# Loading by partition halves on two DMA queues: K, V and weight loads of a decode layer

## The chip, the core and the metric

The kernel runs on one core of one Trainium2 chip. The metric is the device time in microseconds (us) of one execution, the median over several executions. A profile is one further execution taken by the hardware profiler; its span runs from the first to the last instruction on the core, and the execution's own device time is a little longer than its span.

Five engines run beside each other: TensorE (PE, with its weight loads listed as PEld), VectorE (DVE), ScalarE (ACT), GpSimd (POOL) and SyncE (SP). SP and ACT each issue DMAs to a queue of their own; both queues are served by the core's 16 DMA engines.

## What is computed

One decode step of a transformer layer for 4 sequences, one token each, in bfloat16: LayerNorm, attention over the last 2048 positions of a cache with 32 query heads and 4 key/value heads of size 128, then LayerNorm and a gated feed-forward block.

```python
W = min(4096, max(256, Sk // 4))            # 2048
q = (layernorm(x) @ wq).reshape(B, 1, 32, 128)
k = repeat(k_cache[:, :, Sk - W:, :], 8)    # B, 4 -> 32 heads
v = repeat(v_cache[:, :, Sk - W:, :], 8)
p = softmax(q @ k.T * 128 ** -0.5)
h = x + (p @ v).reshape(B, 1, 4096) @ wo
hn = layernorm(h)
out = h + (silu(hn @ w1) * (hn @ w3)) @ w2
```

Shapes: x is 4 x 1024, wq 1024 x 4096, wo 4096 x 1024, w1 and w3 1024 x 3584, w2 3584 x 1024, and each cache gives 4 sequences x 4 heads x 2048 x 128. Every byte of these is read from HBM once, 55.6 MB in all.

## The kernel before

**Where data stands.** One tile, `ring`, takes 160 KiB of each of the 128 partitions. The list `plan` (L128 to L146) says in which order loads are issued and at which place of the ring each lands, in units of `KIB` = 512 elements, which is 1 KiB per partition. `load_next` (L150) issues the next entries of the plan. All of these are issued on SP's queue: wq in two parts, then K of batches 0 to 3, V of batches 0 to 3, wo, w1, w3 in two parts, and w2 in four parts of 17, 7, 3 and 1 rows. A batch of K or V is 2 MB; wo is 8 MB, w1 and w3 7 MB each, w2 7 MB. A load that lands on a place used before waits until the matmuls that read the old data are done, so the calls of `load_next` stand behind those matmuls: `load_next(8)` at the start (L159) covers the plan to the first V entry, one call stands in the wq loop (L267), one in the K loop at its eighth step (L327), two in the PV loop after batches 1 and 3 (L386), one after row 12 of wo (L413), one after wo (L414), and three loads at once in the w1 loop (L463). In SP's own instruction stream they simply follow each other, each with its waits; SP does nothing else. The framework also gives its DMAs eight completion semaphores in turn, so a DMA waits until the eighth one before it has landed.

A DMA of 128 partitions has one contiguous row per partition: 16 KB for a batch of K or V, 64 KB for wo, 56 KB for w1, 28 KB for each half of w3.

**The moved columns.** `CE` = 512 (L111): the last CE columns of the last of a partition's eight wq rows are left out of the tail load (`load_tail`, L122) and come by three small loads (`load_side`, L114) as tiles of 20, 12 and 12 partitions. The projection then adds eight small matmuls for them (L268 to L275). The number of bytes is the same either way; what changes is which DMA engine brings them.

**The order of the work.** Projection q (L251), then 16 steps of the K loop (L309): in each, 16 transposes of K on PE, one copy of half of the result from PSUM by DVE (L319) and one by ACT (L321), and four score matmuls of the step before (L300). Softmax follows (L331 to L357), the PV product over 4 batches x 64 blocks (L376), wo (L403), LayerNorm (L417 to L445), w1 (`gate_up("w1")`, L465), the gate's exponential and reciprocal on ACT and DVE, w3 (`gate_up("w3")`, L472), the product and its transpose on DVE (L474, L477), w2 (L483) and the output.

Of the kernel before, what the change touches and what calls it, by code (L numbers as in the profile page):

```python
# [10 lines left out]
P = 128  # L11
# [8 lines left out]
def kernel(  # L20
# [13 lines left out]
    nc = tc.nc  # L34

    B, _, D = A_x.shape
    Hkv, Sk, Dh = A_k_cache.shape[1], A_k_cache.shape[2], A_k_cache.shape[3]
    Hq = A_wq.shape[1] // Dh
    REP = Hq // Hkv
    W = min(4096, max(256, Sk // 4))  # L40
    F = B_w1.shape[1]
    KC = D // P
    NSB = W // 512
# [30 lines left out]
    PK = P // Hkv  # L74
    JK = W // PK
# [3 lines left out]

    RING = 5 * 16384  # L80
    RQ = 4
    BS = 2
    wq_v = A_wq.rearrange("(p i) n -> p (i n)", i=KC)
    wo_v = A_wo.rearrange("(p i) n -> p (i n)", i=IO)
    w1_v = B_w1.rearrange("(p i) n -> p (i n)", i=KC)
    w3_v = B_w3.rearrange("(p i) n -> p (i n)", i=KC)
    w2_v = B_w2.rearrange("(p i) n -> p (i n)", i=IF)
    ring = stream.tile([P, RING], BF16)
# [4 lines left out]
        nc.sync.dma_start(out=t, in_=src[:, r0 * n : (r0 + m) * n])  # L93
        return [t[:, k * n : (k + 1) * n] for k in range(m)]

    def load_kv(at, src, b):

        out = []
        for k in range(BS):
            v = ring[:, at + k * JK * Dh : at + (k + 1) * JK * Dh]  # L100
            nc.sync.dma_start(
                out=v,
                in_=src[b + k, :, Sk - W : Sk, :].rearrange("g (pp j) d -> pp g (j d)", pp=PK),
            )
            out.append(v.rearrange("p (j d) -> p j d", d=Dh))
        return out

    N_Q, N_F = Hq * Dh, F


    CE = 512  # L111
    SETS = [(0, 5, 4), (80, 3, 2), (104, 3, 2)]

    def load_side(r0, ne, ns):  # L114

        t = ktpool.tile([P, JG * QD * 16], BF16, tag="kT")
        rows = A_wq[r0 * KC : (r0 + ne * 4 * ns) * KC, N_Q - CE : N_Q]
        rows = rows.rearrange("(t i k) n -> k i t n", i=ne, k=KC)[KC - 1]
        nc.sync.dma_start(out=t[: ne * 4, : ns * CE], in_=rows)  # L119
        return [t[: ne * 4, k * CE : (k + 1) * CE] for k in range(ns)]  # L120

    def load_tail(at, src, n, r0, m):  # L122

        t = ring[:, at : at + m * n]
        nc.sync.dma_start(out=t[:, : m * n - CE], in_=src[:, r0 * n : (r0 + m) * n - CE])
        return [t[:, k * n : (k + 1) * n] for k in range(m)]
    KIB = 512
    plan = [  # L128
        ("wq", load_rows, (0, wq_v, N_Q, 0, 4)),
        ("side", load_side, SETS[0]),  # L130
        ("side", load_side, SETS[1]),
        ("side", load_side, SETS[2]),
        ("wq", load_tail, (32 * KIB, wq_v, N_Q, 4, 4)),
        ("k", load_kv, (64 * KIB, A_k_cache, 0)),
        ("k", load_kv, (96 * KIB, A_k_cache, 2)),
        ("v", load_kv, (128 * KIB, A_v_cache, 0)),
        ("v", load_kv, (0, A_v_cache, 2)),
        ("wo", load_rows, (32 * KIB, wo_v, D, 0, 32)),
        ("w1", load_rows, (96 * KIB, w1_v, N_F, 0, 8)),
        ("w3", load_rows, (0, w3_v, N_F, 0, 4)),  # L140
        ("w3", load_rows, (28 * KIB, w3_v, N_F, 4, 4)),
        ("w2", load_rows, (56 * KIB, w2_v, D, 0, 17)),
        ("w2", load_rows, (90 * KIB, w2_v, D, 17, 7)),
        ("w2", load_rows, (104 * KIB, w2_v, D, 24, 3)),
# [5 lines left out]
    def load_next(n=1):  # L150
        for _ in range(n):
            if cursor[0] < len(plan):
                kind, f, args = plan[cursor[0]]
                loaded.setdefault(kind, []).extend(f(*args))
                cursor[0] += 1

    x_sb = act.tile([B, D], BF16)
    nc.scalar.dma_start(out=x_sb[:], in_=x_flat)
    load_next(8)  # L159

    ident = const.tile([P, P], BF16)
    make_identity(nc, ident[:])
# [12 lines left out]
    for c in range(2):  # L175
# [8 lines left out]
        out=xn[:], in0=x_sb[:], scalar1=mv[:, 0:1], scalar2=rstd[:, 0:1],  # L184
# [14 lines left out]
    for r0, ne, ns in SETS:  # L199
        v = xn[:, r0 * KC : (r0 + ne * 4 * ns) * KC]  # L200
        v = v.rearrange("b (s l i k) -> b k l i s", s=4, l=ns, i=ne)
        nc.vector.tensor_copy(
            out=xs[:, len(sl) : len(sl) + ns, : ne * 4].rearrange("b l (i s) -> b l i s", s=4),
            in_=v[:, KC - 1, :, :, :],
        )
        for l in range(ns):
            nc.tensor.transpose(
                out=ts_ps[: ne * 4, len(sl), :], in_=xs[:, len(sl), : ne * 4], identity=ident[:B, :B]
# [4 lines left out]
    for _, ne, ns in SETS:  # L213
# [14 lines left out]
        out=perm[:].rearrange("p (h dq) -> p h dq", dq=JG),  # L228
        in_=ident[:].rearrange("p (dq h) -> p h dq", dq=JG),
# [12 lines left out]
    for j in range(2, JG):  # L242
        nc.vector.tensor_tensor(
            out=same[:, 0, :], in0=same[:, 0, :], in1=ident[:, j * QD : (j + 1) * QD], op=ALU.add
# [6 lines left out]
    for kc in range(KC):  # L251
        wq_t = loaded["wq"][kc]
        for hf in range(CQ // 512):
            for g in range(JG):
                c0 = g * CQ + hf * 512
                n = min(512, N_Q - CE - c0) if kc == KC - 1 else 512
                if n <= 0:
                    continue
                nc.tensor.matmul(  # L259
                    q_ps[QD * g : QD * g + B, hf * 512 : hf * 512 + n],  # L260
                    lhsT=xnT[:, kc, :],
                    rhs=wq_t[:, c0 : c0 + n],
                    start=(kc == 0),
                    stop=(kc == KC - 1 or (kc == KC - 2 and c0 + 512 == N_Q)),
                )
        if kc == RQ - 1:
            load_next()  # L267
            for k, np_ in enumerate(sl):  # L268
                nc.tensor.matmul(
                    q_ps[QD * (JG - 1) : QD * (JG - 1) + B, CQ - CE : CQ],  # L270
                    lhsT=xsT[:np_, k, :],
                    rhs=loaded["side"][k],
                    start=False,
                    stop=False,
                )  # L275
    q_sb = act.tile([P, CQ], BF16)
    nc.vector.tensor_single_scalar(out=q_sb[:, :512], in_=q_ps[:, :512], scalar=qscale, op=ALU.mult)  # L277
# [2 lines left out]
    for r in range(REP):  # L280
        nc.tensor.transpose(out=qt_ps[:, r, :], in_=q_sb[:, r * Dh : (r + 1) * Dh], identity=ident[:])
    nc.vector.tensor_copy(
        out=qz[:, :, : Hkv * QD].rearrange("p b (g z) -> p b g z", g=Hkv)[:, :, :, :REP],
        in_=qt_ps[:].rearrange("p r (g x) -> p x g r", g=Hkv)[:, :B, :, :],
# [10 lines left out]
    def emit_scores(u):  # L295
        b, n = units[u]
        kT_v = kT_tiles[u][:].rearrange("d j (pp g) -> d g j pp", g=Hkv)
        for g in range(Hkv):
            z0 = (b * Hkv + g) * QD
            nc.tensor.matmul(  # L300
                scores_ps[QD * g : QD * (g + 1), n * 512 : (n + 1) * 512],
                lhsT=qz_v[:, z0 : z0 + QD],
                rhs=kT_v[:, g, :, :],
                start=(b == 0),
                stop=(b == B - 1),
            )

    nt = 0
    for u, (b, n) in enumerate(units):  # L309
        k_v = loaded["k"][b]  # L310
        kT = ktpool.tile([P, NJ, P], BF16, tag="kT")
        for t in range(NJ // TB):
            kt_ps = psA.tile([P, TB, P], BF16, tag=f"kt{nt % 4}")
            for jj in range(TB):
                nc.tensor.transpose(  # L315
                    out=kt_ps[:, jj, :], in_=k_v[:, n * NJ + t * TB + jj, :], identity=ident[:]
                )
            if nt % 2 == 0:
                nc.vector.tensor_copy(out=kT[:, t * TB : (t + 1) * TB, :], in_=kt_ps[:])  # L319
            else:  # L320
                nc.scalar.copy(out=kT[:, t * TB : (t + 1) * TB, :], in_=kt_ps[:])  # L321
            nt += 1
        kT_tiles.append(kT)
        if u >= 1:
            emit_scores(u - 1)
        if u == NSB * BS - 1:
            load_next()  # L327
    emit_scores(len(units) - 1)


# [7 lines left out]
        out=Pm[:], in_=scores_ps[:], func=ACT.Exp, bias=nmax[:], scale=1.0, accum_out=rsum[:]  # L338
# [6 lines left out]
    for c in range(NSB):  # L345
# [4 lines left out]
        for g in range(Hkv):  # L350
            if g % 2 == 0:
                nc.vector.tensor_scalar(  # L352
                    out=z[:, :, g, :], in0=pt_ps[:], scalar1=mask[:, g : g + 1], scalar2=None, op0=ALU.mult
# [10 lines left out]
        out=Dm[:], in0=ident[:].rearrange("p (g b r) -> p b g r", g=Hkv, b=B),  # L364
# [11 lines left out]
    for b in range(B):  # L376
        for j in range(JK):
            nc.tensor.matmul(  # L378
                OT_ps[:, b, :],
                lhsT=loaded["v"][b][:, j, :],  # L380
                rhs=PTz[j // NJ][:, (j % NJ) * B + b, :, :],
                start=(j == 0),
                stop=(j == JK - 1),
            )
        if b % BS == BS - 1:
            load_next()  # L386
    OT_sb = act.tile([P, B, Hq], BF16)
    nc.vector.tensor_tensor(out=OT_sb[:], in0=OT_ps[:], in1=bc[:], op=ALU.mult)
# [14 lines left out]
    for i in range(IO):  # L403
        for j in range(JG):
# [5 lines left out]
                stop=(i == IO - 1),  # L410
# [1 line left out]
        if i == 11:  # L412
            load_next()  # L413
    load_next()  # L414


    h1 = act.tile([P, CG], FP32)  # L417
    nc.vector.tensor_tensor(out=h1[:], in0=y_ps[:], in1=x_q[:], op=ALU.add)
# [19 lines left out]
        out=hn[:], in0=h1[:], scalar1=tot[:, 0:1], scalar2=rstd2[:, 0:1],  # L438
# [5 lines left out]
        out=hnT[:].rearrange("p k x -> p (k x)"), in_=hn[:].rearrange("q (c k) -> q k c", k=KC)  # L444
# [5 lines left out]
    def gate_up(kind, out_ps):  # L450
# [27 lines left out]
        out=hgT[:].rearrange("p i x -> p (i x)"),  # L478
        in_=hg[:].rearrange("q s c -> q (s c)").rearrange("q (c i) -> q i c", i=IF),
# [3 lines left out]
    for i in range(IF):  # L483
        for j in range(JG):
# [5 lines left out]
                stop=(i == IF - 1),  # L490
                skip_group_check=True,
# [35 lines left out]
```

## Time and profile before

| what | value |
|---|---|
| device time, median of 3 runs | 138.09 us (137.81 to 138.16) |
| device time of the profiled execution | 138.01 us |
| its span | 136.1 us |
| PE busy / PEld busy | 73.8 us / 45.0 us |
| DVE busy / ACT busy | 43.4 us / 31.1 us |
| read from HBM | 55.59 MB, 408 GB/s over the span |
| packets on SP's data queue (q1) | 2731 |
| instruction fetches (q8) | 8 packets of 16 KB |

The table shows that no compute engine is busy for more than 54% of the span, while the data queue's packets fill nearly all of the time of the 16 DMA engines. "DMA share" in a view by stages is the mean busy share of these 16 engines; it can exceed 1.00 in a short stage, because a packet is counted in the stage in which it starts.

### The profile page before, as it was taken

How to read it: one execution, taken by the hardware profiler on the slowest of the kernel's cores; microseconds unless marked ns; L12 is line 12 of the kernel's file. 1: busy time of each engine (PE TensorE's matmuls, PEld its weight loads, DVE VectorE, ACT ScalarE, POOL GpSimd, SP SyncE). 2: the span in 40 equal slices, each digit the busy share in tenths (PEclk: the TensorE clock that was granted, in tenths of full speed). 3: DMA queues.
4: the chain of work that ended last, by engine and by line, in shares of the span. 5: the costliest groups of instructions: out<-in, count | busy, mean ns of one | idle time of the engine just before them, and what ended most of it. 6: DMA issues, size and time to landing. Idle time of an engine off the chain costs nothing.

```text
span 136.1 us, 2343 instructions
## 1 busy us (share of the span) xinstructions
PE 73.8 (54%) x1050; PEld 45.0 (33%) x1050; DVE 43.4 (32%) x79; ACT 31.1 (23%) x36; POOL 1.7 (1%) x8
## 2 busy tenths in 40 slices
PE   0202980979898989810535906793096440900960
PEld 0200220267474747400024905571043210300840
DVE  6820000044243434471984001206100695080000
ACT  3000000016555555518385200000002300000001
POOL 5000000000000000000000000000000000000000
PEclk9999999999999999997555555579757777555577
DMA  5999999999999999999979999989899999989970
GB/s 156 463 464 404 404 438 405 424 428 438 433 428 419 429 443 428 429 522 477 462 327 443 481 409 404 477 371 477 354 430 426 438 455 442 430 389 419 421 288 5
DMA packets 2789, 55.75 MB, mean 410 GB/s; under 512 B 311, under 2 KB 471, under 8 KB 731
## 3 DMA queue, kind: packets, MB, share of 16 engines
q1 hardware_dynamic: 2731, 55.58, 95.6%
q8 instruction: 8, 0.13, 0.3%
q10 hardware_dynamic: 48, 0.02, 0.1%
q14 instruction: 2, 0.02, 0.0%
HBM read 55.59 MB, written 0.01 MB: 408 GB/s over the span
## 4 chain that ended last, share of the span: by engine, by line
DMA 54%; PE 24%; ACT 11%; DVE 5%; SPq 2%; issue 1%; ACTq 0%
DMA ring<-in_B_w_dram 40%; DMA ring<-in_A_wq_dram 15%; PE kt_ps L315 10%; ACT kT L321 5%; PE scores_ps L300 5%; ACT z L356 3%; PE q_ps L259 3%; SPq L119 2%; PE g_ps L455 2%; DVE rmax L332 2%; ACT Pm L337 2%; PE OT_ps L378 2%; DVE pT L346 1%; DVE z L352 1%; ACT L337 1%
## 5 line engine op out<-in xcount | busy, mean ns | idle before, releaser
L321 ACT COPY kT<-kt_ps 128x1024 bf16<-128x1024 bf16 x16 | 15.9, 1013 | 13.1 <-PE kt_ps L315 13.1
L315 PE MATMUL kt_ps<-ident,ring 128*128 128x128 bf16 x256 | 17.8, 230 | 0.0
L315 PEld LDWEIGHTS <-ring 128*128 128x128 bf16 x256 | 15.8, 104 | 4.9 <-issue 4.9
L319 DVE COPY kT<-kt_ps 128x1024 bf16<-128x1024 bf16 x16 | 11.1, 692 | 16.2 <-PE kt_ps L315 16.2
L259 PE MATMUL q_ps<-ring,xnT 128*4 128x512 bf16 x63 | 7.2, 626 | 10.5 <-DMA ring<-in_A_wq_dram 10.5
L378 PE MATMUL OT_ps<-z,ring 128*128 128x32 bf16 x256 | 7.5, 188 | 9.0 <-ACT z L356 5.0
L455 PEld LDWEIGHTS <-hnT 128*32 128x32 bf16 x128 | 5.3, 137 | 19.3 <-issue 16.6
L300 PE MATMUL scores_ps<-kT,qz 128*32 128x512 bf16 x64 | 9.9, 610 | 2.9 <-ACT kT L321 2.9
L455 PE MATMUL u_ps<-ring,hnT 128*32 128x448 bf16 x64 | 6.4, 576 | 8.2 <-DMA ring<-in_B_w_dram 8.2
L378 PEld LDWEIGHTS <-ring 128*128 128x128 bf16 x256 | 7.4, 105 | 9.8 <-issue 9.7
L485 PE MATMUL y_ps<-ring,hgT 128*32 128x256 bf16 x112 | 5.8, 375 | 8.3 <-DMA ring<-in_B_w_dram 8.1
L455 PE MATMUL g_ps<-ring,hnT 128*32 128x448 bf16 x64 | 5.5, 529 | 5.2 <-DMA ring<-in_B_w_dram 5.2
L485 PEld LDWEIGHTS <-hgT 128*32 128x32 bf16 x112 | 4.5, 130 | 10.2 <-issue 5.9
L259 PEld LDWEIGHTS <-xnT 128*4 128x4 bf16 x63 | 2.0, 115 | 14.8 <-issue 14.7
L277 DVE TENSOR_SCALAR q_sb<-q_ps 128x512 bf16<-128x512 f32 x1 | 0.7, 692 | 19.5 <-PE q_ps L259 19.5
L495 ACT CAST res<-y_ps 128x256 bf16<-128x256 f32 x1 | 0.4, 372 | 26.4 <-PE y_ps L485 26.4
L356 ACT ACTIVATE z<-pt_ps,mask 128x512 bf16<-128x512 f32 x8 | 5.3, 687 | 3.5 <-DVE z L352 3.5
L348 PE MATMUL pt_ps<-pT,perm 128*128 128x512 bf16 x4 | 2.4, 608 | 6.8 <-DVE pT L346 6.8
L278 ACT ACTIVATE q_sb<-q_ps 128x512 bf16<-128x512 f32 x1 | 0.6, 597 | 23.6 <-DVE q_sb L277 23.6
L405 PE MATMUL y_ps<-ring,o 128*32 128x256 bf16 x128 | 5.5, 352 | 0.8 <-DVE o L394 0.8
L352 DVE TENSOR_SCALAR z<-pt_ps,mask 128x512 bf16<-128x512 f32 x8 | 5.5, 738 | 1.2 <-ACT z L356 0.8
L469 DVE RECIPROCAL eg<-eg 128x896 f32<-128x896 f32 x1 | 5.8, 5754 | 0.0
(79 smaller groups left out, 50.2 us busy)
## 6 DMA issues: line engine op xcount, KB each, us to landing
ring<-in_A_k_cache_dram SPq DMA_DIRECT2D x4, 2048.0 KB, 25.4
ring<-in_A_v_cache_dram SPq DMA_DIRECT2D x4, 2048.0 KB, 39.0
ring<-in_B_w_dram SPq DMA_DIRECT2D x1, 7168.0 KB
ring<-in_B_w_dram SPq DMA_DIRECT2D x2, 3584.0 KB, 23.3
ring<-in_B_w_dram SPq DMA_DIRECT2D x1, 4352.0 KB
ring<-in_A_wq_dram SPq DMA_DIRECT2D x1, 4096.0 KB, 12.1
ring<-in_A_wq_dram SPq DMA_DIRECT2D x1, 3968.0 KB, 19.8
ring<-in_B_w_dram SPq DMA_DIRECT2D x1, 1792.0 KB
```

The lines of the kernel that those rows point to most:

```text
L259: nc.tensor.matmul(q_ps[QD * g : QD * g + B, hf * 512 : hf * 512 + n], lhsT=xnT[:, kc, :], rhs=wq_t[:, c0 : c0 + n], start=(kc == 0), stop ...
L300: nc.tensor.matmul(scores_ps[QD * g : QD * (g + 1), n * 512 : (n + 1) * 512], lhsT=qz_v[:, z0 : z0 + QD], rhs=kT_v[:, g, :, :], start=(b = ...
L315: nc.tensor.transpose(out=kt_ps[:, jj, :], in_=k_v[:, n * NJ + t * TB + jj, :], identity=ident[:])
L319: nc.vector.tensor_copy(out=kT[:, t * TB : (t + 1) * TB, :], in_=kt_ps[:])
L321: nc.scalar.copy(out=kT[:, t * TB : (t + 1) * TB, :], in_=kt_ps[:])
L352: nc.vector.tensor_scalar(out=z[:, :, g, :], in0=pt_ps[:], scalar1=mask[:, g : g + 1], scalar2=None, op0=ALU.mult)
L356: nc.scalar.mul(out=z[:, :, g, :], in_=pt_ps[:], mul=mask[:, g : g + 1])
L378: nc.tensor.matmul(OT_ps[:, b, :], lhsT=loaded["v"][b][:, j, :], rhs=PTz[j // NJ][:, (j % NJ) * B + b, :, :], start=(j == 0), stop=(j == J ...
L405: nc.tensor.matmul(y_ps[QD * j : QD * (j + 1), :], lhsT=o4[:, i, :, :].rearrange("p b s -> p (b s)"), rhs=loaded["wo"][i][:, j * CG : (j + ...
L455: nc.tensor.matmul(out_ps[QD * j : QD * (j + 1), hf, :HF], lhsT=hnT[:, k, :], rhs=loaded[kind][k][:, c0 : c0 + HF], start=(k == 0), stop=( ...
L469: nc.vector.reciprocal(out=eg[:], in_=eg[:])
L485: nc.tensor.matmul(y2_ps[QD * j : QD * (j + 1), :], lhsT=hgT[:, i, :], rhs=loaded["w2"][i][:, j * CG : (j + 1) * CG], start=False, stop=(i ...
```

## The change

From the third batch of K to w3, each load is issued as two DMAs of 64 partitions: the lower half on SP's queue, the upper half on ACT's. K of batches 0 and 1, wq and w2 stay single DMAs of 128 partitions on SP. The calls of `load_next` are spread over the K loop: two loads at step 0 and one each at steps 3, 6, 9, 11 and 13, behind that step's copy. w3 becomes one load of eight rows per partition where it was two of four; it is issued after row 12 of wo. `CE` is 352 where it was 512, so the last wq row keeps 160 more columns and the eight small matmuls have 352 columns; one matmul of 160 columns joins the projection.

In ACT's stream this puts two DMA issues behind its first K copy, then one each behind its copies 4, 7, 10, 12 and 14, and two (w1, w3) between the last softmax product and the second LayerNorm's square root. The order of all other instructions on PE, DVE, ACT and POOL is unchanged.

```diff
+    def load_halves(at, src, n, r0, m):
+        t = ring[:, at : at + m * n]
+        for q, (p0, p1) in ((nc.sync, (0, P // 2)), (nc.scalar, (P // 2, P))):
+            tc.keep_in_program_order(
+                q.dma_start(out=t[p0:p1, :], in_=src[p0:p1, r0 * n : (r0 + m) * n])
+            )
+        return [t[:, k * n : (k + 1) * n] for k in range(m)]
+
+    def load_kv(at, src, b, parts):
+        v = ring[:, at : at + JK * Dh]
+        rows = src[b, :, Sk - W : Sk, :].rearrange("g (pp j) d -> pp g (j d)", pp=PK)
+        n = PK // len(parts)
+        for k, q in enumerate(parts):
+            tc.keep_in_program_order(
+                q.dma_start(
+                    out=v[k * n * Hkv : (k + 1) * n * Hkv, :],
+                    in_=rows[k * n : (k + 1) * n],
+                )
+            )
+        return [v.rearrange("p (j d) -> p j d", d=Dh)]
...
-    CE = 512
+    CE = 352
...
+    one, two = (nc.sync,), (nc.sync, nc.scalar)
...
-        ("k", load_kv, (64 * KIB, A_k_cache, 0)),
-        ("k", load_kv, (96 * KIB, A_k_cache, 2)),
-        ("v", load_kv, (128 * KIB, A_v_cache, 0)),
-        ("v", load_kv, (0, A_v_cache, 2)),
-        ("wo", load_rows, (32 * KIB, wo_v, D, 0, 32)),
-        ("w1", load_rows, (96 * KIB, w1_v, N_F, 0, 8)),
-        ("w3", load_rows, (0, w3_v, N_F, 0, 4)),
-        ("w3", load_rows, (28 * KIB, w3_v, N_F, 4, 4)),
+        ("k", load_kv, (64 * KIB, A_k_cache, 0, one)),
+        ("k", load_kv, (80 * KIB, A_k_cache, 1, one)),
+        ("k", load_kv, (96 * KIB, A_k_cache, 2, two)),
+        ("k", load_kv, (112 * KIB, A_k_cache, 3, two)),
+        ("v", load_kv, (128 * KIB, A_v_cache, 0, two)),
+        ("v", load_kv, (144 * KIB, A_v_cache, 1, two)),
+        ("v", load_kv, (0, A_v_cache, 2, two)),
+        ("v", load_kv, (16 * KIB, A_v_cache, 3, two)),
+        ("wo", load_halves, (32 * KIB, wo_v, D, 0, 32)),
+        ("w1", load_halves, (96 * KIB, w1_v, N_F, 0, 8)),
+        ("w3", load_halves, (0, w3_v, N_F, 0, 8)),
...
-    load_next(8)
+    load_next(7)
...
         if kc == RQ - 1:
-            load_next()
...
-        if u == NSB * BS - 1:
-            load_next()
+        load_next({0: 2, 3: 1, 6: 1, 9: 1, 11: 1, 13: 1}.get(u, 0))
...
-        if b % BS == BS - 1:
+        if b == 1:
             load_next()
```

More of the change, by code (lines that the diff above doesn't have):

```diff
@@ L81 @@
     RQ = 4
-    BS = 2
     wq_v = A_wq.rearrange("(p i) n -> p (i n)", i=KC)
@@ L94, in load_rows @@
         return [t[:, k * n : (k + 1) * n] for k in range(m)]
[L96 to L103, printed above, removed]
-            )
-            out.append(v.rearrange("p (j d) -> p j d", d=Dh))
-        return out
+    def load_halves(at, src, n, r0, m):
[3 more added lines that the diff above has]
+                q.dma_start(out=t[p0:p1, :], in_=src[p0:p1, r0 * n : (r0 + m) * n])
+            )
+        return [t[:, k * n : (k + 1) * n] for k in range(m)]
[11 more added lines that the diff above has]
+        return [v.rearrange("p (j d) -> p j d", d=Dh)]
     N_Q, N_F = Hq * Dh, F
-    CE = 512
+    CE = 352
     SETS = [(0, 5, 4), (80, 3, 2), (104, 3, 2)]
@@ L263 @@
                     start=(kc == 0),
-                    stop=(kc == KC - 1 or (kc == KC - 2 and c0 + 512 == N_Q)),
+                    stop=(kc == KC - 1),
+                    skip_group_check=(c0 + 512 == N_Q),
                 )
         if kc == RQ - 1:
-            load_next()
             for k, np_ in enumerate(sl):
@@ L274 @@
                     stop=False,
+                    skip_group_check=True,
                 )
```

## The prediction

> **What bounds the kernel now.** I read the shares by queue and the slices first, then the DMA share by stages, then the chain of waits, then the order of time around the places that the change touches.
>
> ```profile
> DMA  5999999999999999999979999989899999989970
> q1 hardware_dynamic: 2731, 55.58, 95.6%
> q8 instruction: 8, 0.13, 0.3%
> 2.00:130.00 128.00, 71.77 (x1006) 43.64 (x1007) 42.36 (x77) 30.72 (x35) 0.29 (x2) 0.79 1.00 427
> 130.00:132.80 2.80, 1.73 (x40) 1.24 (x40) 0.00 (x0) 0.00 (x0) 0.00 (x0) 0.83 0.68 266
> ```
>
> The fourth line is one stage from 2 to 130 us: after the busy times of PE, PEld, DVE, ACT and POOL and PE's clock stands the DMA share, 1.00, at 427 GB/s. So the 16 DMA engines never pause there, whatever the compute engines wait for. In the last 2.8 us the share is 0.68: some engines are done, others not. If all ended together, at most 0.32 x 2.8 = 0.9 us would be won. That is the whole room for a change that moves the same bytes at the same rate.
>
> ```profile
> 75.97 22.91 DMA ring<-in_B_w_dram
> 98.92 2.41 PE g_ps L455 x17
> 101.46 31.31 DMA ring<-in_B_w_dram
> ```
>
> The chain of waits ends in two DMA pieces of 54 us together. They are issue-to-landing, so most of each is queueing behind earlier loads. The last load lands at 132.77; four matmuls, a copy and the output follow (3.3 us), which the change leaves alone. Compute matters only if it issues a load too late, or is late itself at the end:
>
> ```profile
> 30.97 1.01 ACT L321 COPY kT<-kt_ps 128x1024 bf16<-128x1024 bf16 x1 [2.40 <-PE kt_ps L315]
> 32.41 1.01 ACT L321 COPY kT<-kt_ps 128x1024 bf16<-128x1024 bf16 x1 [0.43 <-PE kt_ps L315]
> ...
> 82.35 2.05 PE L378 MATMUL OT_ps<-z,ring 128*128 128x32 bf16 x70 [4.01 <-issue]
> ...
> 115.83 3.18 PE L455 MATMUL u_ps<-ring,hnT 128*32 128x448 bf16 x32 [5.27 <-DMA ring<-in_B_w_dram]
> 119.06 1.09 DVE L474 TENSOR_TENSOR hg<-u_ps,gs 128x896 bf16<-128x896 f32 x1 [4.67 <-PE u_ps L455]
> 120.18 1.70 DVE L477 STREAM_TRANSPOSE hgT<-hg 128x896 bf16<-128x896 bf16 x1
> 126.09 3.82 PE L485 MATMUL y_ps<-ring,hgT 128*32 128x256 bf16 x68 [7.08 <-DMA ring<-in_B_w_dram]
> 130.34 1.22 PE L485 MATMUL y_ps<-ring,hgT 128*32 128x256 bf16 x28 [0.43 <-DMA ring<-in_B_w_dram]
> ```
>
> In brackets stands the idle time before the work and what ended it. After w3's second part lands, PE and DVE need 6.05 us (115.83 to 121.88) and then wait for w2 until 126.09.
>
> The packet records add three things. A 16 KB row takes 611 ns, a 64 KB row 2418: 27.2 GB/s per engine plus some 9 ns a row. While ACT's small x_q load ran beside wq (6 to 11 us), each of its 512-byte packets came after one whole 32 KB row of SP's queue and took 27 ns; the row kept its 1213 ns. So an engine takes rows from the two queues by turns, at no visible cost. And each of PE's eight 16 KB instruction fetches takes 0.88 to 0.96 us on one engine, where most also lengthen the next row by 0.47 to 0.55: an engine so hit runs 1.4 us behind. The side loads put three others about as far behind, two less. In the last landing 4 engines are done at 130.97 to 131.64, 12 at 132.40 to 132.77.
>
> [...]
>
> **The change part by part.**
>
> *Moved columns.* 160 columns x 2 bytes return to each partition's row: 8 rows an engine x 320 bytes = 2.6 KB, at 27.2 GB/s +0.09 us on every engine. The three engines with most side bytes (32 rows of 1024 bytes, now 704) lose 10.2 KB: net -0.28 us. The fetch-hit engines, which also end late, take the +0.09, so the end moves by +0.09. The tail load may land some 0.3 us earlier (23.57 before); one more matmul of 160 columns, about 0.2 us, eats most of that, all under the DMA stream.
>
> *Eight more loads in halves.* Same bytes, same rows per engine. K 2 and 3, V, wo and w1 each add one completion write of 9 ns on an engine: 8 x 9 = +0.07 us. w3 as one load has 8 rows of 2116 ns where 16 of 1062 stood: 8 x 8 ns = -0.06 us.
>
> *Issues on ACT.* SP's issues of such loads took 535 to 635 ns. The two behind ACT's first copy cost 1.2 us, and 0.43 of idle time stood there: +0.8 us on the K loop, whose chain passes through ACT's copies. Those behind copies 4, 7, 10, 12 and 14 meet gaps of 1.75, 0.55, 0.78, 1.75 and 0.78 us: +0.1. Semaphore waits of these issues end earlier (V 2's upper half needs K 3's, landing near 44.6, and stands at 47). w1's and w3's upper halves stand before the square root, which needs wo's end anyway. So w1's issue (75.97, behind PV of batch 1) becomes about 76.9. The stream would run dry at 80.06, when wo lands on the first engine, and an issue took 1.0 us to its first packet: 2 us are left. Cost 0; past that cover it is one to one.
>
> *w3 as one load.* Its issue waits for row 12 of wo: 89.0 before, where its first half went at 84.0. PE's 4.01 us stop in PV is an instruction fetch that waited behind 64 KB rows; behind two queues it may wait one row longer, +2.4 us, so w3 goes at about 92. w1 ends on the earliest engine at 97.0: 5 us are left. Cost 0.
>
> *Lag of the upper half.* ACT can issue K 2's upper half only at 32.0, first packet 33.0 to 33.4, but K 1 is done at 31.6 on the earliest engines: SP's lower half runs alone for up to 1.8 us, 3 rows. By turns the upper stays 3 rows behind until SP runs out after wo (near 70, w1's slot not free); ACT's rest then catches up to about 1 row by 78. With 1 row, w3's upper part ends behind one 34 KB row of w2 (1.29 us): 117.1. Now 64 matmuls follow, not 32: 6.2 us, then the same 2.9, so w2 starts at 126.2, where its data sets 126.09. Cost 0.1 at that place, gone by 130.34. Three rows would mean 119.7 and a start at 128.8.
>
> Sum on the DMA end: +0.09 + 0.07 - 0.06 = +0.10. Profiled execution: 138.01 + 0.10 = 138.1; the median shown is 0.08 above it, so 138.2.
>
> **Unknown prices.** *A fetch with two busy queues*: the 0.5 us lengthening may vanish if the other queue's row fills it, or stay; -0.5 to 0, taken 0. *The 9 ns per row*: 72 rows of halves per engine; hidden entirely -0.65, doubled +0.65; taken 0, as x_q's turns cost nothing. [...] Taken 0, because nothing in before shows two engines holding each other up, but this is the least sure value here.
>
> **Rivals.**
> 1. *Faster*: the second queue fills fetch bubbles and row gaps. For: 12 of 16 engines end late. Against: the share is already 1.00. -0.3 (fetches, less on the engine hit at 130.38) - 0.65 + 0.1 = -0.85: 137.3.
> 2. [...] Place: K 2 lower alone, 1.8 us, and wo's upper rest alone, about 7 us. At half rate 4.4 us are lost: 142.4; with less lag 139. [...] Against: alternation uses both halves. It decides once engines write the same half's rows together for more than 0.8 us.
> 3. *The same in full*: [...] Signs: 16 KB rows well above 611 ns.
> 4. *w3's lag stays at 3 rows*: +1 to 2, 139 to 140.
>
> **Numbers.** No change to speak of, 0.34 (own range 137.7 to 138.6); faster 0.20; rivals 2 and 4 0.30, at 139 to 142.5; rival 3 0.16. A measurement tells 0.3%, 0.41 us, from no change. The range 137.2 to 142.5 leaves out rival 3 and a little at the ends. Faster 0.21, same 0.31, slower 0.48: the slower cases together outweigh, but each alone is less likely than 138.2.
>
> **What would show it.** Right: share 1.00 to about 130, rows of 611 and 2418 ns on both queues, last landing near 132.9, w3 near 117, w2's first matmul near 126.2. The moved columns: wq's tail landing slightly earlier. Wrong: [...] a dip in the share near 80 or 97 (w1 or w3 issued late), w2's matmuls starting after 127 and the last landing not the end (lag), or next rows after fetches no longer lengthened and the 12 late engines earlier (rival 1).

## The result and the profile after

The changed kernel takes 220.85 us (median of 4 runs, 217.92 to 222.04) where the kernel before takes 138.01: ratio 1.587, 95% interval 1.573 to 1.601. The ratios here and below leave out executions that took over 1.5% more than the fastest of the same kernel, here two of four, the profiled one among them, so this ratio sets 219.0 us against 138.0: 81 us more. The profiled execution took 221.56 us, its span is 219.8.

The lines of the page that answer to those shown of before, from the profile of the changed kernel (DMA share and GB/s in 40 slices, then the data queues of SP, q1, and of ACT, q10):

```profile
DMA  7999999999999999999999999999899999978991
GB/s 288 413 438 427 420 382 212 265 248 251 259 239 259 270 194 206 239 228 209 218 198 224 245 206 219 188 188 240 191 219 209 209 243 188 216 126 317 408 411 40
q1 hardware_dynamic: 2011, 37.75, 60.0%
q10 hardware_dynamic: 768, 17.85, 37.1%
```

The first line looks as before: the 16 DMA engines are busy throughout. The second tells the story. From slice 7 (33 us), where the third batch of K begins, to slice 36 the same busy engines move about half as much; wq and the first batches of K before that, and w2 after it, run at the old rate. The share says how busy the engines are and not how fast; the rate of the 16 engines while busy is GB/s divided by the share. By stages of the changed kernel (the last two columns are DMA share and GB/s):

```profile
4.00:31.00 27.00, 13.64 (x116) 6.53 (x117) 5.29 (x24) 1.05 (x3) 0.00 (x0) 1.00 0.98 421
33.00:36.00 3.00, 2.36 (x39) 2.07 (x38) 1.78 (x3) 1.36 (x2) 0.00 (x0) 1.00 1.07 218
40.00:76.00 36.00, 20.95 (x206) 13.39 (x204) 8.67 (x11) 14.11 (x14) 0.00 (x0) 0.77 1.00 254
100.00:180.00 80.00, 14.33 (x261) 9.82 (x261) 5.73 (x16) 3.78 (x4) 0.00 (x0) 0.56 1.01 214
203.00:212.00 9.00, 6.07 (x92) 3.34 (x88) 2.79 (x2) 0.00 (x0) 0.00 (x0) 0.69 0.96 411
```

421 / 0.98 is 430 GB/s on 128 partitions; 218 / 1.07 is 204 while SP's lower half of K 2 runs alone; 254 while 16 KB rows of both halves take turns, 212 with rows of 56 and 64 KB. The packet records agree row by row: 64 KB rows take 4.72 to 6.66 us (2.42 before), w1's and w3's 56 KB rows mostly 4.2 to 4.5 (2.12 before), 16 KB rows mostly 0.9 to 1.27 where 0.61 stood, on both queues.

The slices 7 to 36 last 165 us and have 220 GB/s in the mean, so 36.3 MB move in them. At 432 GB/s, between the 429 and 434 that 16 engines give with before's rows of 611 ns (16 KB) and 2418 ns (64 KB), these would take 84 us: 81 us are lost here, of the 83.6 between the profiled executions. The chain of waits of the changed kernel shows where it is felt:

```profile
31.48 25.07 DMA ring<-in_A_k_cache_dram
62.30 48.33 DMA ring<-in_A_v_cache_dram
113.63 29.90 another core or an unknown queue
151.47 19.29 another core or an unknown queue
173.44 42.93 DMA ring<-in_B_w_dram
```

The two "unknown" pieces end as wo's and w1's last marks arrive (143.54 and 170.77): PE waits there for weights. PE's busy time hardly grows (75.7 us, 73.8 before); PE waits for loads instead.

### The profile page after: what moved, and what is told of

Read it like the earlier page. It is cut to its first block, busy times and chain, and to the rows that moved or that the text cites. A ratio compares the mean times of both kernels' runs of the same rounds, so it can differ in the third digit from the quotient of the medians.

```text
span 219.8 us, 2367 instructions
## 1 busy us (share of the span) xinstructions
PE 75.7 (34%) x1051; PEld 47.6 (22%) x1051; DVE 43.4 (20%) x79; ACT 31.4 (14%) x36; POOL 1.7 (1%) x8
## 2 busy tenths in 40 slices
DMA packets 2789, 55.75 MB, mean 254 GB/s; under 512 B 439, under 2 KB 599, under 8 KB 859
## 4 chain that ended last, share of the span: by engine, by line
DMA 62%; another core or an unknown queue 22%; PE 11%; SPq 1%; DVE 1%; issue 1%; ACT 0%; DVEq 0%; ACTq 0%
DMA ring<-in_A_v_cache_dram 22%; DMA ring<-in_B_w_dram 20%; DMA ring<-in_A_k_cache_dram 11%; DMA ring<-in_A_wq_dram 9%; PE y_ps L419 3%; PE kt_ps L330 3%; PE q_ps L273 2%; SPq L129 1%; PE g_ps L468 1%; PE OT_ps L392 1%; PE scores_ps L315 1%; PE qt_ps L296 1%; DVE q_sb L292 0%; ACT kT L336 0%
## 5 line engine op out<-in xcount | busy, mean ns | idle before, releaser
L330 PE MATMUL kt_ps<-ident,ring 128*128 128x128 bf16 x256 | 22.9, 255 | 10.1 <-DMA ring<-in_A_k_cache_dram 9.3
L330 PEld LDWEIGHTS <-ring 128*128 128x128 bf16 x256 | 19.1, 116 | 17.2 <-DMA ring<-in_A_k_cache_dram 9.9
L468 PE MATMUL u_ps<-ring,hnT 128*32 128x448 bf16 x64 | 5.1, 501 | 25.8 <-DMA ring<-in_B_w_dram 25.8
L392 PEld LDWEIGHTS <-ring 128*128 128x128 bf16 x256 | 7.4, 104 | 26.1 <-issue 26.0
L419 PEld LDWEIGHTS <-o 128*32 128x32 bf16 x128 | 4.9, 131 | 31.7 <-issue 31.1
L498 PE MATMUL y_ps<-ring,hgT 128*32 128x256 bf16 x112 | 5.1, 339 | 4.4 <-DVE hgT L490 2.9
L481 DVE TENSOR_SCALAR eg<-eg 128x896 f32<-128x896 f32 x1 | 0.6, 627 | 24.9 <-ACT eg L480 24.9
```

What stands on the lines that cost most here:

```text
L330: nc.tensor.transpose(out=kt_ps[:, jj, :], in_=k_v[:, n * NJ + t * TB + jj, :], identity=ident[:])
L392: nc.tensor.matmul(OT_ps[:, b, :], lhsT=loaded["v"][b][:, j, :], rhs=PTz[j // NJ][:, (j % NJ) * B + b, :, :], start=(j == 0), stop=(j == J ...
L419: nc.tensor.matmul(y_ps[QD * j : QD * (j + 1), :], lhsT=o4[:, i, :, :].rearrange("p b s -> p (b s)"), rhs=loaded["wo"][i][:, j * CG : (j + ...
L468: nc.tensor.matmul(out_ps[QD * j : QD * (j + 1), hf, :HF], lhsT=hnT[:, k, :], rhs=loaded[kind][k][:, c0 : c0 + HF], start=(k == 0), stop=( ...
L498: nc.tensor.matmul(y2_ps[QD * j : QD * (j + 1), :], lhsT=hgT[:, i, :], rhs=loaded["w2"][i][:, j * CG : (j + 1) * CG], start=False, stop=(i ...
```

## Experiments

Theory 1 is the prediction's third rival: engines that write partitions of one half at the same time, whether from one queue or from two by turns, get about half the rate (204 to 254 GB/s in the stages above, 430 on 128 partitions). Its rivals: taking turns between two queues costs the rate (theory 2), any DMA of 64 partitions is slow (theory 3), or the moved columns do it.

**Two queues, split by columns.** Each DMA of a pair spans 128 partitions. K and V, whose lines are left out here, are split by columns likewise.

```diff
-        for q, (p0, p1) in ((nc.sync, (0, P // 2)), (nc.scalar, (P // 2, P))):
+        h = m * n // 2
+        for k, q in enumerate((nc.sync, nc.scalar)):
...
-                q.dma_start(out=t[p0:p1, :], in_=src[p0:p1, r0 * n : (r0 + m) * n])
+                q.dma_start(
+                    out=t[:, k * h : (k + 1) * h],
+                    in_=src[:, r0 * n + k * h : r0 * n + (k + 1) * h],
+                )
...
```

> As the changed kernel, with its two queues, its places of issue and its 352 columns, but each pair of DMAs splits a load by columns: both DMAs span all 128 partitions. Theory 1 [...]: rows at full rate again, 16 KB in about 0.61 us per 16 KB, DMA rate near 430 GB/s, time 138 to 139 us. Theory 2 (taking turns between two queues costs the rate): still near 217 GB/s in these stages, about 220 us.

142.25 us (140.80 to 143.53); ratio 1.026 (1.019 to 1.034). From 2 to 130 us its stage view shows the full rate:

```profile
2.00:130.00 128.00, 66.22 (x939) 39.09 (x939) 40.30 (x76) 31.01 (x35) 0.29 (x2) 0.76 1.00 427
```

Theory 2 falls: two queues by turns move 427 GB/s. But some 4 us are left, where at most 1 was expected. The chain of waits of this run places them:

```profile
86.66 39.34 DMA ring<-in_B_w_dram
126.05 3.20 PE u_ps L472 x32
129.27 1.10 DVE hg L491
130.40 1.71 DVE hgT L494
132.15 4.93 PE y_ps L502 x112
```

w3's last part lands at 126.0, ten microseconds later than before, and all 112 matmuls of w2 come after 132.15, with no wait for w2's data among them. In the packet records SP's part of w3 ends at 111.9 us and w2's rows begin at 104.7, while ACT's part of w3 runs to 125.1. That is the fourth rival, the lag of one queue behind the other, in a kernel with more rows.

**The same, with w3 on SP alone.** The edit also moves w3's first issue back to its place in the kernel before.

```diff
-        ("w3", load_halves, (0, w3_v, N_F, 0, 8)),
+        ("w3", load_rows, (0, w3_v, N_F, 0, 4)),
+        ("w3", load_rows, (28 * KIB, w3_v, N_F, 4, 4)),
...
-        if b == 1:
+        if b % 2 == 1:
             load_next()
```

> As the column split on two queues, with w3 again as two loads of four rows per partition on SP alone, issued behind PV of batch 3 and behind row 12 of wo. Theory (the column split lost its 4 us because ACT's part of w3 was taken by turns with w2 and landed at 126 us): w2's matmuls start by 127 us and the time is 138.3 to 139.5 us. Rival (two queues cost the DMA stream itself some us): last landing and time stay near 141 to 142 us.

138.65 us (138.43 to 138.80); ratio 1.0050 (1.0035 to 1.0065). In its order of time w2 waits for its own data again:

```profile
126.58 3.82 PE L503 MATMUL y_ps<-ring,hgT 128*32 128x256 bf16 x68 [8.57 <-DMA ring<-in_B_w_dram]
```

By the two ratios, w3's lag cost some 3 us of 3.6; this is rough, as the times of the column split spread over 2.7 us. The rest, +0.7 us (+0.5 to +0.9), fits the price of a row: the page counts 3941 packets where the kernel before, with its longer rows, has 2789; 1152 / 16 engines x 9 ns = 0.65 us. By this sum the second queue does not hide it.

**One queue, halves kept.** Both halves go on SP.

```diff
-(nc.scalar, (P // 2, P))
+(nc.sync, (P // 2, P))
...
-    one, two = (nc.sync,), (nc.sync, nc.scalar)
+    one, two = (nc.sync,), (nc.sync, nc.sync)
```

> As the changed kernel, but both halves of each load go on the SP queue, one behind the other; ACT issues none of them. Theory 1: [...] 35.7 MB at 217 GB/s take 164 us in place of 83, so about 218 us as before the experiment. Theory 2: with one queue no turns, so about 138 us.

224.07 us, somewhat above the 218 expected; ratio 1.623 (1.616 to 1.630). By stages:

```profile
40.00:76.00 36.00, 20.86 (x261) 12.97 (x258) 16.89 (x25) 18.55 (x22) 0.00 (x0) 0.82 1.01 228
100.00:180.00 80.00, 12.23 (x196) 7.87 (x196) 7.76 (x13) 2.50 (x3) 0.00 (x0) 0.56 1.00 207
```

The loss needs no second queue. Two queues even help a little: 254 against 228 GB/s in the first stage, 214 against 207 in the second.

**wo alone in halves**, all else as before, both on SP (partitions 0 to 63, then 64 to 127).

```diff
-        ("wo", load_rows, (32 * KIB, wo_v, D, 0, 32)),
+        ("wo", load_parts, (32 * KIB, wo_v, D, 0, 32)),
...
+        for q, p0, p1 in ((nc.sync, 0, 64), (nc.sync, 64, 128)):
...
+                q.dma_start(out=t[p0:p1, :], in_=src[p0:p1, r0 * n : (r0 + m) * n])
...
```

> The kernel before with one load changed: wo comes as partitions 0 to 63, then 64 to 127, both on SP. Theory 1: 8.4 MB at 217 in place of 432 GB/s, +19.3 us, about 157 us; 64 KB rows of about 4.8 us. Theory 3 (any DMA of 64 partitions is slow, wherever its partitions lie): the same 157 us, to be compared with the next run. Theory 2: 138 us.

163.86 us; ratio 1.187 (1.184 to 1.191), +25.9 where 19.3 were expected. The stage of wo:

```profile
64.00:98.00 34.00, 9.92 (x262) 7.95 (x262) 8.15 (x15) 6.81 (x10) 0.00 (x0) 0.50 1.03 211
```

211 / 1.03 is 205 GB/s. Its rows take 4.8 to 5.1 us for the most part (median near 5.1): 8 rows an engine x 2.7 us is 21.6. The neighbours of wo are slowed too: w1's first rows, which some engines begin while others still write wo's upper half, take up to 5.8 in place of 2.1 us.

**wo in the middle.** The list of parts becomes partitions 32 to 95, 0 to 31, 96 to 127.

```diff
-        for q, p0, p1 in ((nc.sync, 0, 64), (nc.sync, 64, 128)):
+        for q, p0, p1 in ((nc.sync, 32, 96), (nc.sync, 0, 32), (nc.sync, 96, 128)):
```

> The kernel before with wo as partitions 32 to 95, then 0 to 31, then 96 to 127, all on SP. Theory 1: [...] only the two quarters, half of the bytes, run at half rate, +9.6 us, about 147.7 us, with 64 rows of 64 KB near 2.42 us and 64 near 4.8 us. Theory 3: all rows near 4.8 us or slower, 157 us or more.

153.06 us; ratio 1.109 (1.107 to 1.111); 147.7 were expected, with slow rows of 4.8 us and no rows slowed at the borders. The stages of the 64 middle partitions and of the two quarters:

```profile
60.00:66.00 6.00, 1.79 (x3) 0.34 (x4) 3.14 (x6) 3.33 (x4) 0.00 (x0) 0.50 1.18 511
72.00:90.00 18.00, 6.16 (x209) 5.71 (x208) 1.65 (x4) 1.97 (x2) 0.00 (x0) 0.50 0.98 198
```

511 / 1.18 is 433 GB/s, 198 / 0.98 is 202. In the packet records 56 of the first 64 rows take 2418 ns to the nanosecond; the other 8, at the border to the next DMA, take longer, and all later rows about 5.1 us. A DMA of 64 rows on the same queue runs at full speed at partitions 32 to 95 and at half speed at 0 to 63: theory 3 falls. The middle lies on both sides of partition 64.

**Read side or write side?** The same three destinations are filled from other rows of wo: the middle takes rows 0 to 63 of the source, so wo's product becomes another one.

```diff
-        for q, p0, p1 in ((nc.sync, 32, 96), (nc.sync, 0, 32), (nc.sync, 96, 128)):
+        for p0, p1, s0 in ((32, 96, 0), (0, 32, 64), (96, 128, 96)):
...
-                q.dma_start(out=t[p0:p1, :], in_=src[p0:p1, r0 * n : (r0 + m) * n])
+                nc.sync.dma_start(
+                    out=t[p0:p1, :], in_=src[s0 : s0 + p1 - p0, r0 * n : (r0 + m) * n]
+                )
...
```

> As the run with wo in partitions 32 to 95, 0 to 31 and 96 to 127, but the 64 partitions from 32 to 95 are filled from wo's rows of partitions 0 to 63, and the others from the rest: rows of wo reach the wrong partitions, so wo's product is another one; bytes and instructions are the same. Write side (theory 1): the same 153 us, 64 rows at 2.42 us. Read side (it is the HBM rows of partitions 0 to 63 that cannot be read fast by 16 engines): those 64 rows near 5 us and the time at 160 us or more.

153.19 us; ratio 1.110 (1.108 to 1.112), and the same two groups of rows, 57 of the first 64 at 2418 ns. The stage of the middle partitions:

```profile
60.00:66.00 6.00, 1.79 (x3) 0.34 (x4) 3.13 (x6) 3.33 (x4) 0.00 (x0) 0.50 1.20 519
```

519 / 1.20 is 433 GB/s. The source does not matter here. In these runs the limit lies on the write side: with partitions 32 to 95 as destination both sources give 433 GB/s, and rows 0 to 63 of wo, slow at partitions 0 to 63 (205 GB/s over the two halves), are fast here.

**Which 64 or 16 partitions?** wo as even, then odd partitions, and wo as eight DMAs of 16 partitions, 8 apart, all on SP. The diff is that of step 2; for step 8 the loop runs over range(8) with a step of 8.

```diff
-        for q, p0, p1 in ((nc.sync, 0, 64), (nc.sync, 64, 128)):
+        for p0 in (0, 1):
...
-                q.dma_start(out=t[p0:p1, :], in_=src[p0:p1, r0 * n : (r0 + m) * n])
+                nc.sync.dma_start(out=t[p0:P:2, :], in_=src[p0:P:2, r0 * n : (r0 + m) * n])
...
```

> The kernel before with wo as the even partitions, then the odd ones, both on SP: each DMA has 64 partitions[...]. Theory 1a [...]: all 64 KB rows at 2.42 us, 138 us. Theory 1b [...]: rows near 5 us as in the run with wo in halves, about 164 us.

> The kernel before with wo as eight DMAs of 16 partitions, 8 apart, on SP: each engine has one row of each DMA, whichever engine takes which. [...] rows take near 5 us, about 160 us in all. [...] rows take 2.42 us and the time is 138 us.

Step 2: 138.07 us, ratio 1.0007 (0.9998 to 1.0016). Step 8: 160.3 us, ratio 1.161 (1.157 to 1.165). The stage of wo, first with step 2, then with step 8:

```profile
62.00:78.00 16.00, 8.28 (x192) 6.16 (x192) 8.27 (x14) 7.61 (x12) 0.00 (x0) 0.50 1.01 435
```

```profile
64.00:96.00 32.00, 10.59 (x263) 8.14 (x263) 9.60 (x17) 6.85 (x11) 0.00 (x0) 0.50 1.01 214
```

Of two readings of theory 1, the one that goes by which partitions a DMA has (1a) fits step 2: every row takes 2418 ns but one, right after an instruction fetch. The other (1b) went by which engines write at the same moment, assumed that each engine takes four rows of the DMA in a row, in step with the others, and predicted rows near 5 us for step 2 that do not occur; so one of these assumptions is wrong for this shape, and how the 64 rows are dealt out stays open. With step 8 every engine has one row per DMA (each DMA leaves 16 completion marks in the packet records), so no order of dealing can help, and rows take about 5 us. Its 16 partitions lie in both halves too, as those of step 2 and of the middle do; so lying in both halves is not enough, and what sets step 8 apart is not shown.

**The moved columns alone.** The kernel before with 352 for 512.

```diff
-    CE = 512
+    CE = 352
```

> The kernel before with 352 moved columns and nothing else. Theory 1 gives the whole loss to the halves: 138.1 us, within 0.3% of before (+0.09 us by the sum in the prediction). Rival: the narrower side loads unbalance the engines for the rest of the kernel, then clearly over 138.4 us.

138.05 us; ratio 1.0001 (0.9993 to 1.0009). On their own they do nothing that can be measured.

**The change with other halves.** The changed kernel, only that SP takes the even partitions and ACT the odd ones.

```diff
-        for q, (p0, p1) in ((nc.sync, (0, P // 2)), (nc.scalar, (P // 2, P))):
+        for k, q in enumerate((nc.sync, nc.scalar)):
...
-                q.dma_start(out=t[p0:p1, :], in_=src[p0:p1, r0 * n : (r0 + m) * n])
+                q.dma_start(out=t[k:P:2, :], in_=src[k:P:2, r0 * n : (r0 + m) * n])
...
-                    out=v[k * n * Hkv : (k + 1) * n * Hkv, :],
-                    in_=rows[k * n : (k + 1) * n],
...
+            tc.keep_in_program_order(q.dma_start(out=v[k:P:n, :], in_=rows[:, k:Hkv:n]))
...
```

> The changed kernel with one thing other: the two halves of a load are the even partitions (SP) and the odd ones (ACT) in place of the lower and the upper. Two queues, 64 partitions a DMA, 352 columns and all places of issue stay. Theory 1 [...]: rows at 611, 2418 and 2116 ns on both queues, the loss of 83 us gone but for w3's lag, 138.5 to 143 us. Rival (two queues and 64 partitions together cost it): near 220 us.

138.17 us (137.95 to 138.41, 12 runs), a little below the range expected; ratio 1.0011 (1.0002 to 1.0020). The loss is gone, with two queues, 64 partitions a DMA and every place of issue as in the change:

```profile
2.00:130.00 128.00, 68.12 (x1007) 42.21 (x1008) 42.26 (x77) 31.01 (x35) 0.29 (x2) 0.77 1.00 427
130.00:132.80 2.80, 1.34 (x40) 1.06 (x40) 0.00 (x0) 0.00 (x0) 0.00 (x0) 1.00 0.67 264
```

**The same with w3 on SP alone**, edited as in the second experiment.

> As the run before with even and odd partitions, and w3 as two loads of four rows on SP alone, at the places of the kernel before. If what was left is w3's lag: 138.0 to 138.8 us. If the two queues still cost the stream something: as the run before it.

138.21 us; ratio 1.0014 (1.0007 to 1.0022). Here w3's lag was already small, so nothing was left to win. No version beat the kernel before: its DMA stream is full from 2 to 130 us, and none of these moves fewer bytes.

## Why the prediction was wrong

**The step that failed** is the price of engines that slow each other when they write one half together: "Taken 0, because nothing in before shows two engines holding each other up". In the change, 16 engines write DMAs of 64 partitions of one half each, and they move 204 to 254 GB/s in place of 432: +81 us. The third rival, that the loss stays while the queues take turns, was right, and its sign came: 16 KB rows mostly at 0.9 to 1.27 us where 0.61 stood, 214 GB/s in the longest stage. It was given 0.16 and left outside the range. One reading led there: ACT's x_q load was taken as evidence that such engines do not slow each other, though its 16 partitions are 8 apart, the very pattern that halves the rate for 64 KB rows (step 8). But its packets are 512 bytes and take 27 ns, and in the packet records they come in four trains of four, one packet every 1.23 us, so presumably on four engines: they had hardly a chance to meet. Where a trace has no case of a thing, its silence does not make the price 0.

**The second rival**, half the rate for a half that is written alone, had half of the reach: a lone half does run at half rate (218 / 1.07 = 204 GB/s at 33 us). What it had wrong is that alternation would help because it uses both halves. It does use both: from 40 to 76 us eight engines in the mean are on each queue, at 254 GB/s. And a nearly empty half is no faster. From 105.2 to 109.7 us at most four of the 16 engines have rows of the upper half, of wo, and these still take 4.97 to 5.05 us where 2.42 stood before. So it is not simply the number of engines in a half that counts; what does is not shown, as the records do not have which engine writes which partition. 16 KB rows were held up less (254 GB/s) than long ones (214); why, stays open as well.

**The rest of the sum held**, as far as it can be seen, in the even/odd run, which differs from the change only in the choice of partitions. Predicted 138.2, measured 138.17; that the two agree to 0.03 us is in part luck, as the single terms, 0.06 to 0.1 us each, are below what these runs tell apart. Its order of time, in place of the predicted 117.1 for w3, 126.2 for w2's first matmul and 132.9 for the last landing:

```profile
101.26 5.28 PE L463 MATMUL g_ps<-ring,hnT 128*32 128x448 bf16 x64 [9.21 <-DMA ring<-in_B_w_dram]
117.23 5.82 PE L463 MATMUL u_ps<-ring,hnT 128*32 128x448 bf16 x64 [10.68 <-DMA ring<-in_B_w_dram]
126.22 3.57 PE L493 MATMUL y_ps<-ring,hgT 128*32 128x256 bf16 x68 [3.17 <-DMA ring<-in_B_w_dram]
130.45 0.95 PE L493 MATMUL y_ps<-ring,hgT 128*32 128x256 bf16 x28 [0.66 <-DMA ring<-in_B_w_dram]
```

w3's matmuls start at 117.23, and the last piece of w2 lands at 132.87. The +0.10 us of the sum lies inside this run's interval (+0.03 to +0.28 us). The moved columns, priced at +0.09, cannot be told from 0 (-0.10 to +0.12).

**Issues on ACT** were priced too high, at +0.8 us on the K loop. In the even/odd run:

```profile
29.83 1.01 ACT L331 COPY kT<-kt_ps 128x1024 bf16<-128x1024 bf16 x1 [1.48 <-PE kt_ps L325]
29.84 1.25 ACTq L110 DMA_DIRECT2D ring<-in_A_k_cache_dram  x2
31.13 1.01 ACT L331 COPY kT<-kt_ps 128x1024 bf16<-128x1024 bf16 x1 [0.29 <-issue]
```

The two issues run beside the copy that they stand behind in the stream, and only 0.29 us of idle time is left before the next copy, less than the 0.43 of before. The K loop ended at 57.9 us, before at 58.3. w1's issue came at 75.6, where 76.9 was predicted.

**The first rival** fell: rows after fetches are still about 0.5 us longer (2611 to 2622 ns for 2116 on ACT's queue in the even/odd run), and the column split's +0.7 us fits a row price of 9 ns paid in full.

**The fourth rival** shows in the change too, though it did not set the end there. The lower rows of w3 ended at 182.9 us and the upper ones at 200.0, while w2's rows had begun at 187.7. So w2's matmuls began only at 210.12, having waited for w3's product (2.93 us) and not for data; but the last of them still waited for w2's last piece, which landed at 216.37. In the even/odd run w3 came when one row of lag had been predicted; in the column split the lag cost some 3 us.

## What to carry to other kernels

If a load must be split over queues, split it by columns or into even and odd partitions (427 GB/s each from 2 to 130 us), and not into partitions 0 to 63 and 64 to 127 (214 to 254 by turns on two queues); here no split was faster than whole loads on one queue. Read DMA share and GB/s together: a share of 1.00 went with 427 GB/s and with 254. When two queues share the engines, the part that was issued later can stay behind, which cost some 3 us in the column split and nothing that could be measured in the even/odd run; so a load that the end of the kernel waits for is safer on one queue.

## What the runs showed of the hardware

Two DMAs of the same 64 rows of wo differ by a factor of two through their destination alone: 433 GB/s at partitions 32 to 95 (the run with other source rows), 205 where wo comes as partitions 0 to 63, then 64 to 127. Rows at half rate took slightly more than twice as long: 64 KB rows took about 5.1 us where twice 2.42 is 4.84. DMAs of 16 partitions 8 apart ran at half rate (214 GB/s), DMAs of 64 partitions 2 apart at the full one (435). And a DMA issue on ACT overlaps the copy ahead of it: two issues, 1.25 us, beside a copy of 1.01 us.
